# Reading the first expert's early rows two units sooner

## The chip, the cores and the metric

The program runs on one core of a Trainium2 chip. The metric is the time of one execution on the device, in microseconds (us). The kernel before took 737.21 us (median of 3 runs, 736.69 to 739.57).

## The reference

Three stages follow each other: an mLSTM over 4 batches, 8 heads and 768 steps; a mixture of 8 experts in which each of the 3072 tokens goes to the one expert with the highest logit; and a gated MLP over all tokens. Shortened, with the names of the reference:

```python
for t in range(S):                                   # mLSTM, per batch and head
    m_new = max(f_gate[t] + m, i_gate[t])
    f, i = exp(f_gate[t] + m - m_new), exp(i_gate[t] - m_new)
    C = f * C + i * outer(v[t], k[t]);  n = f * n + i * k[t]
    y[t] = sigmoid(o_gate[t]) * (C @ q[t]) / max(abs(n @ q[t]), 1)

logits = (x / |x|) @ (emb / |emb|).T / tau           # x: 3072 x 320
expert = argmax(logits);  gate = max(softmax(logits))
out[expert == e] = gate * (relu(x[expert == e] @ w1[e]) @ w2[e])   # 320 -> 1024 -> 320

h = x @ w_in;  result = (h * sigmoid(1.702 * h)) @ w_out           # 320 -> 2048 -> 320
```

## The kernel before, in words

**Units.** The mLSTM is cut into 24 units of 128 tokens (6 pieces of the sequence, 4 batches), worked on in one loop over `u` = 0 to 23; the last one, 23, and what follows it are written out behind the loop (the tail). Every engine runs its own queue in the order in which the code is written: nothing is reordered by a scheduler. In a unit, TensorE (PE) makes scores and products, VectorE (DVE) a scan and the elementwise work, ScalarE (ACT) copies, and GpSimd (POOL) the outputs `x` of a unit (`finish`) and the scatters.

**Routing.** Two units later a unit's rows are transposed (`route_t`), its 8 logits are made (`route_l`), and per batch of units come the one-hot of the best expert (`route_hot`), the rank inside the expert (`route_rank`, small matmuls into the single PSUM bank `r`), the slot (`route_slot`) and the running count of rows per expert (`route_cnt`). A `scatter` on POOL then writes the 128 rows of a unit to their slots in the DRAM tensor `rows`, which holds a region per expert. Scatters run behind by some units: `pend` holds those still to come.

**The first expert.** At `u` = 8 the expert with the most rows so far is named the first. Its first 256 rows (`EARLY`) are worked on ahead of the others: `early_load` reads them from `rows` into a buffer of SBUF, `early_x(c)` transposes them in three parts of 128 columns, `early_xhi` and `early_xlo` split each part into a rounded half (`xeh`) and the remainder (`xel`), and `early_mm(s, i0, i1)` makes the products of hidden block `s` (6 blocks of 128, 8 matmuls each: five with `xeh`, three with `xel`). `early_relu` makes their activations `he`. These products stand between the last routing steps of the tail.

**Sorting and the flag.** `order` sorts the experts by their counts, with some 20 short operations of DVE on 8 or 64 numbers, and writes `vals_i`: the experts in order, where their rows go, and a flag. The flag is 1 if an expert has more rows than was planned for it, or if the first expert had less than 256 rows when they were read (`enough`); then every engine takes a slow general path. All engines load the flag into a register and branch.

**Behind the sort.** `load_x0(1)` reads rows 256 to 511 of the first expert (tile `xr`), `early_o(m)` multiplies hidden block `m` by the second weights (6 matmuls each), then comes the branch, `touch` and the transposes of `xr` (`prep_x0`), and from there the experts one after the other. `xr` lies in memory that the first stage used; so its load waits for the last instructions that used that memory, among them the tiny ACT operation on `warm` that follows two table loads of ACT (one for the square root `rn` of the rows' norms, one for Exp).

In the loop the changed lines stand in this surrounding:

```python
for u in range(0, NU - 1):                 # NU = 24
    ...                                    # scores, scan, epilogues, routing of unit u - 2
    for i in range(0 if u < US else 1 if u < NU - 5 else 2):     # US = 10
        if pend:
            scatter(pend.pop(0))
```

Of the kernel before, what the change touches and what calls it, by code (L numbers as in the profile page):

```python
# [14 lines left out]
ALU = mybir.AluOpType  # L15
# [11 lines left out]
def kernel(ctx, tc, qT_in, kT_in, kvo_in, i_gate, f_gate, expert_emb, tau, w12, wio, out, dbg=None):  # L27
# [116 lines left out]
    with ExitStack() as actx:  # L144
# [116 lines left out]

        dC = ps_o.tile([P, G, 3 * DV], F32, tag="dC", name="dC")
        nc.vector.memset(dC, 0.0)
# [347 lines left out]

        def route_l(u, late=None):
# [6 lines left out]
            nc.tensor.matmul(lp, xT[:, 2], enT[:, 2], start=False, stop=True)  # L619
            if late in (None, 1):  # L620
# [31 lines left out]
        def route_hot(us):  # L652
            for _ in hot_steps(us):
                pass
# [17 lines left out]

        def route_cnt(us):
            oh, old, new = hot.pop(us[0])
            cs = wk.tile([P, E], F32, tag="cs", name="cs")
            nc.vector.tensor_reduce(out=cs, in_=oh.rearrange("p n e -> p e n"), axis=AX.X, op=ALU.add)
            nc.vector.tensor_tensor(out=new, in0=old, in1=cs, op=ALU.add)

        def route_slot(us, late=False):
# [64 lines left out]
        onehot = ap1.tile([P, E], F32, name="onehot")  # L744
        lack = const.tile([P, 1], F32, name="lack")

        def first():
# [14 lines left out]

        def enough(out):

            t = wk.tile([P, E], F32, tag="cs", name="cs")
            nc.vector.tensor_tensor(out=t, in0=early["n"], in1=onehot, op=ALU.mult)
            yield
            nc.vector.tensor_reduce(out=lack, in_=t, axis=AX.X, op=ALU.add)
            yield
            nc.vector.tensor_scalar(out=out, in0=lack, scalar1=-1.0, scalar2=float(EARLY), op0=ALU.mult, op1=ALU.add)  # L770
# [10 lines left out]
        def early_n():  # L781
            early["b"] = ps_o.tile([P, H, NI], F32, tag="ip", name="xt").rearrange("p h d -> p (h d)")

            early["n"] = early["b"][:, EARLY:EARLY + E]
            nc.tensor.matmul(early["n"], ones16, cnt[(nroute[0] - 1) % 2], start=True, stop=True)

        def early_x(c):
            if c == 0:
                early["h"] = wk.tile([P, 3, EARLY], F32R, tag="xeh", name="xeh", bufs=1)
                t = wk.tile([P, H, P], F32R, tag="wm", name="xel").rearrange("p h t -> p (h t)")  # L790
                early["l"] = t[:, 0:3 * EARLY].rearrange("p (c t) -> p c t", c=3)
            if c == 1:
                early["b"] = ps_o.tile([P, H, NW], F32, tag="op", name="xt").rearrange("p h d -> p (h d)")
            t = early["t", c] = early["b"][:, c // 2 * EARLY:(c // 2 + 1) * EARLY]
# [9 lines left out]
        def early_mm(s, i0=0, i1=8):  # L804
            if s == 0 and i0 == 0:
                early["p", 0] = ps_1.tile([P, H, P], F32, tag="sp", name="hp").rearrange("p h t -> p (h t)")[:, 0:EARLY]
            elif s == 1 and i0 == 0:
                early["p", 1] = dC.rearrange("p g f -> p (g f)")[:, 0:EARLY]
            elif 1 < s < 4 and i0 == 0:
                early["p", s] = ps_t.tile([P, G, P], F32, tag="pt", name="hp").rearrange("p a t -> p (a t)")[:, 0:EARLY]  # L810
            elif s == 4:
                early["p", s] = ps_o.tile([P, H, NW], F32, tag="op", name="hp").rearrange("p h d -> p (h d)")[:, 0:EARLY]
            elif s == 5:
                early["p", s] = ps_o.tile([P, H, NI], F32, tag="ip", name="hp").rearrange("p h d -> p (h d)")[:, 0:EARLY]
            h_seq(early["p", s], wslot[s][0], early["h"], early["l"], i0, i1)

        def early_relu(s):
# [11 lines left out]
            else:  # L829
                nc.vector.scalar_tensor_tensor(out=hl, in0=hp, scalar=0.0, in1=hh.bitcast(F32), op0=ALU.max, op1=ALU.subtract)  # L830

        def order_mm():
            early["a"] = r_bank(2)[:, 0:E]
            nc.tensor.matmul(early["a"], ones16, cnt[nroute[0] % 2], start=True, stop=True)

        def order():
# [10 lines left out]
            bg, q, m1, m2, m3, m4 = (sq(i, j) for i in range(2) for j in range(3))  # L847
            lacks = enough(cp[:, E:E + 1])
            nc.vector.tensor_copy(cn, early["a"])
            next(lacks)  # L850
            nc.vector.scalar_tensor_tensor(out=key, in0=cn, scalar=float(E), in1=key0, op0=ALU.mult, op1=ALU.add)
            tt(out=bg, in0=row(key), in1=col(key), op=ALU.is_gt)
            next(lacks)
            red(ordr, bg)
# [3 lines left out]
            tt(out=m3, in0=q, in1=row(cn), op=ALU.mult)  # L858
            next(lacks, None)
            red(cp[:, 0:E], m3)  # L860
# [11 lines left out]
        with tc.manual_schedule():  # L872
# [45 lines left out]
            for u in range(0, NU - 1):  # L918
# [117 lines left out]
            for i in pend:  # L1036
                scatter(i)
            early_load()
            pv(u - 1)
# [10 lines left out]
            assert next(steps, True)  # L1050
            keep_warm(dC.rearrange("p g f -> p (g f)"), 2)
            route_sq(u - 1)
# [7 lines left out]
            early_n()  # L1060
# [6 lines left out]
            early_x(0)  # L1067
            route_l(u, 1)
            route_rank(batch, 2)
            route_slot(batch, True)  # L1070
            route_cnt(batch)
            for i in batch:
                scatter(i)
            early_x(1)
            early_x(2)
            for c in range(3):
                early_xhi(c)
            nc.scalar.activation(out=rn, in_=ss_all.unsqueeze(2), func=AF.Sqrt)
            nc.scalar.activation(out=warm, in_=warm, func=AF.Exp)
            batch = [u]  # L1080
            route_hot(batch)
            early_mm(0, 0, 5)
            route_rank(batch, 2)
            early_xlo(0)
            route_slot(batch, True)
            route_cnt(batch)
            for i in batch:
                scatter(i)
            for c in range(1, 3):
                early_xlo(c)  # L1090
            for s in range(1, 4):
                early_mm(s, 0, 5)
                if s == 2:
                    order_mm()
# [631 lines left out]
```

## Time and profile before

| | |
|---|---|
| median of 3 runs | 737.21 us (736.69 to 739.57) |
| the profiled execution's own time | 739.55 us |
| its span, first to last instruction | 737.9 us |
| mean granted TensorE clock | 0.994 of full speed |
| the tail, from the last unit's scores to `touch` | 157.52 to 183.41 us of the span |
| PE busy in the span | 714.6 us (97%), 4767 matmuls |
| DVE, ACT, POOL busy | 515.3, 368.3, 237.6 us |

A row of the timeline reads: start, length, engine, line, operation, tiles (output, arrow, inputs), shape, number of instructions; in brackets, how long the engine sat idle ahead of it and what ended that. A row with more than one instruction runs from the first one's start to the last one's end. The granted clock (PEclk) of a stretch is a share of full speed.

### The profile page before, as it was taken

What the parts mean: (1) busy time and instruction counts of PE and PEld (TensorE: products, weight loads), DVE (VectorE), ACT (ScalarE), POOL (GpSimd) and SP (SyncE); (2) the same over time, 40 slices, a digit from 0 to 9 for tenths busy, and PEclk for the clock granted to TensorE, in tenths of its full rate; (3) what the DMA queues carried; (4) which work ended last, traced back from release to release, by engine and by line L of the source; (5) the groups of instructions that cost most, each with busy time, mean ns of one, the idle gap of its engine ahead of it and who ended that gap; (6) DMA issues with size and microseconds to landing.
All of it is one profiled execution on the core that took longest, in us unless ns stands there. A gap on an engine that the chain in (4) does not pass through costs nothing.

```text
span 737.9 us, 13402 instructions
## 1 busy us (share of the span) xinstructions
PE 714.6 (97%) x4767; PEld 669.6 (91%) x4767; DVE 515.3 (70%) x1080; ACT 368.3 (50%) x857; POOL 237.6 (32%) x353
## 2 busy tenths in 40 slices
PE   7999999997999999999999999999999999999994
PEld 5899899997989999999998888888888888889994
DVE  8778899985799998999867745545645544435542
ACT  4664555544666665767555443433333333334442
POOL 6674678873235433645210003003003003002011
PEclk9999999999999999999999999999999999999998
DMA  5689988822877768677721202202201201102000
GB/s 174 200 287 269 284 233 261 250 88 78 288 238 158 236 193 221 193 222 242 215 64 57 71 1 58 65 0 58 65 1 52 48 1 48 33 0 57 3 20 18
DMA packets 70106, 93.14 MB, mean 126 GB/s; under 512 B 31858, under 2 KB 56530, under 8 KB 70034
## 3 DMA queue, kind: packets, MB, share of 16 engines
q1 hardware_dynamic: 66818, 84.05, 39.3%
q0 software_dynamic: 3072, 7.89, 3.1%
q8 instruction: 38, 0.62, 0.4%
q14 instruction: 34, 0.28, 0.1%
q10 hardware_dynamic: 144, 0.30, 0.1%
HBM read 71.11 MB, written 17.18 MB: 120 GB/s over the span
## 4 chain that ended last, share of the span: by engine, by line
issue 43%; PE 24%; POOL 5%; DVE 2%; DMA 1%; POOLq 0%; ACT 0%; SPq 0%
PE acc L1225 12%; PE hp L139 11%; POOL out_dram L1270 3%; POOL xr L1381 2%; PE xt L1149 1%; DMA xr<-y 1%; DVE w L122 0%; POOL gap L1272 0%; DVE xl L1151 0%; DVE w L112 0%; DVE hs L1199 0%; DVE fr L1294 0%; PE xt L1165 0%; POOLq L1721 0%; DVE ex L1291 0%
## 5 line engine op out<-in xcount | busy, mean ns | idle before, releaser
L1225 PE MATMUL acc<-wout,hhl 128*128 128x320 f32 x1152 | 187.3, 309 | 0.0
L1225 PEld LDWEIGHTS acc<-wout,hhl 128*128 128x128 f32 x1152 | 175.9, 188 | 7.8 <-DVE o L1252 0.2
L1210 DVE TENSOR_TENSOR sg<-hp,sg 128x512 f32<-128x512 f32 (+1 forms) x112 | 68.9, 615 | 93.5 <-ACT sg L1209 85.9
L139 PE MATMUL hp<-xh,win 128*128 128x512 f32 (+1 forms) x560 | 131.1, 364 | 0.0
L1270 POOL DMA_INDIRECT out_dram<-o,tokd x24 | 24.0, 1002 | 312.9 <-ACT o L1254 309.2
L1209 ACT ACTIVATE sg<-hp 128x512 f32<-128x512 f32 (+1 forms) x112 | 60.4, 539 | 124.5 <-PE hp L139 121.9
L1212 DVE TENSOR_TENSOR hhl<-sg,hhl 128x512 fp32r<-128x512 f32 (+1 forms) x112 | 71.7, 640 | 70.3 <-ACT hhl L1211 69.8
L1225 PE MATMUL acc<-w,hs 128*128 128x320 f32 x636 | 104.3, 310 | 0.7 <-DVE hs L1199 0.7
L139 PEld LDWEIGHTS hp<-xh,win 128*128 128x128 f32 x560 | 93.8, 188 | 11.7 <-DVE sg L1210 0.3
L1211 ACT CAST hhl<-sg 128x512 fp32r<-128x512 f32 (+1 forms) x112 | 62.7, 559 | 80.5 <-DVE sg L1210 78.2
L1225 PEld LDWEIGHTS acc<-w,hs 128*128 128x128 f32 x636 | 96.8, 188 | 2.5 <-DVE hs L1199 1.0
L139 PE MATMUL hp<-xl,win 128*128 128x512 f32 (+1 forms) x336 | 85.7, 363 | 0.0
L111 POOL TENSOR_TENSOR w<-r,w 128x256 fp32r<-128x256 f32 x58 | 49.5, 853 | 102.9 <-ACT w L106 78.4
L139 PEld LDWEIGHTS hp<-xl,win 128*128 128x128 f32 x336 | 58.8, 189 | 11.0 <-DVE xl L1421 0.2
L139 PE MATMUL hp<-xh,w 128*128 128x440 f32 (+6 forms) x320 | 66.8, 338 | 0.0
L139 PEld LDWEIGHTS hp<-xh,w 128*128 128x128 f32 x320 | 51.4, 189 | 1.7
L1198 ACT ACTIVATE hs<-hp 128x440 fp32r<-128x440 f32 (+6 forms) x64 | 30.3, 473 | 38.2 <-PE hp L139 36.4
L479 PE MATMUL sp<-qT,kblk 120*128 120x128 f32 x384 | 47.1, 276 | 0.2 <-DVE wm L484 0.2
L479 PEld LDWEIGHTS sp<-qT,kblk 120*128 120x128 f32 x384 | 44.8, 192 | 0.9 <-issue 0.5
L542 PE MATMUL op<-vp_in,wm 128*128 128x96 f32 (+1 forms) x368 | 43.7, 272 | 0.0
L542 PEld LDWEIGHTS op<-vp_in,wm 128*128 128x128 f32 x368 | 42.9, 192 | 0.0
L139 PE MATMUL hp<-xl,w 128*128 128x440 f32 (+6 forms) x192 | 42.8, 331 | 0.0
(323 smaller groups left out, 1127.0 us busy)
## 6 DMA issues: line engine op xcount, KB each, us to landing
r<-in_w_dram SPq DMA_DIRECT2D x32, 704.0 KB
kvo<-in_kvo_dram SPq DMA_DIRECT2D x24, 480.0 KB
c<-in_wio_dram SPq DMA_DIRECT2D x16, 704.0 KB
fb<-dec SPq DMA_DIRECT2D x40, 128.0 KB
rows<-zt SPq DMA_DIRECT2D x8, 640.0 KB
qT<-in_qT_dram SPq DMA_DIRECT2D x24, 180.0 KB
xr<-y SPq DMA_DIRECT2D x5, 640.0 KB
kblk<-in_kT_dram SPq DMA_DIRECT2D x48, 60.0 KB
```

The source lines that it names most:

```text
L111: eng.tensor_tensor(out=t[:, 3 * P:5 * P].rearrange("p (c f) -> p c f", c=2), in0=r1[:, 0:2], in1=hif[:, 0:2], op=ALU.subtract)
L139: nc.tensor.matmul(hp, a, b, start=(i == 0), stop=(i == len(seq) - 1))
L479: nc.tensor.matmul(sp[:, h - hs.start], kblk[u % NLD][0:KR, h // 3, h % 3, :], qT[u][0:KR, h // 3, :], start=True, stop=True)
L542: nc.tensor.matmul(ops[:, h * NW:h * NW + n], wm[u][:, h], vp_in[u % NLD][:, h * DV:h * DV + n], start=True, stop=True)
L1198: nc.scalar.activation(out=hh, in_=hp, func=AF.Relu)
L1209: nc.scalar.activation(out=sg, in_=hp, func=AF.Sigmoid, scale=1.702)
L1210: nc.vector.tensor_tensor(out=g, in0=hp, in1=sg, op=ALU.mult)
L1211: nc.scalar.copy(hh, g)
L1212: nc.vector.tensor_tensor(out=hl, in0=g, in1=hh.bitcast(F32), op=ALU.subtract)
L1225: nc.tensor.matmul(acc_t[blk][i], hl if j == 2 else hh, w[:, DM:2 * DM] if j == 1 else w[:, 0:DM], start=(first and j == 0), stop=(last an ...
L1270: sc = nc.gpsimd.indirect_dma_start(out=out, out_offset=bass.IndirectOffsetOnAxis(ap=tokd[:, ti:ti + 1], axis=0), in_=o[:, i], in_offset=None)
L1381: eng.tensor_tensor(out=xr_t[blk], in0=xr_t[blk], in1=gated[:, t0:t0 + n].unsqueeze(2).to_broadcast([P, n, 3 * P]), op=ALU.mult)
```

## The change

- `early_load` moves from the tail (behind all scatters so far) to the end of the loop's body at `u` = 21, and reads into a buffer of the `kvo` pool that unit 20 has done with. By then the scatters of units 0 to 15 have been issued: on odd `u` from 11 to 17 the loop now issues two, and one from 18 to 21.
- `enough` moves from the sort to `u` = 20: a small matmul of the counts into bank `r` and three DVE operations that write `miss`. An ACT copy brings `miss` into the sort.
- In the tail, `early_x` takes the place of matmuls of the identity whose results nothing reads (`keep_warm`, L84), and parts of `early_mm` stand between the last logits. Units 22 and 23 get their one-hots one behind the other, then their ranks and slots.
- The square root `rn` and the Exp on `warm` move from ahead of the activations `early_relu` to behind them.
- The load of the flag moves behind `early_o`.

```diff
-        def enough(out):
+        def enough():
+            n = r_bank(None)[:, 0:E]
+            nc.tensor.matmul(n, ones16, cnt[nroute[0] % 2], start=True, stop=True)
             t = wk.tile([P, E], F32, tag="cs", name="cs")
-            nc.vector.tensor_tensor(out=t, in0=early["n"], in1=onehot, op=ALU.mult)
+            nc.vector.tensor_tensor(out=t, in0=n, in1=onehot, op=ALU.mult)
...
         def early_load():
-            t = pmb[0].rearrange("p h t -> p (h t)")
+            t = ld.tile([P, 3, H, D], F32, tag="kvo", name="er", bufs=4).rearrange("p a h d -> p (a h d)")
...
-                for i in range(0 if u < US else 1 if u < NU - 5 else 2):
+                for i in range(0 if u < US else 1 + u % 2 if u < 18 else 1 if u < NU - 2 else 2):
                     if pend:
                         scatter(pend.pop(0))
+                if u == NU - 4:
+                    enough()
+                if u == NU - 3:
+                    early_load()
...
             for i in pend:
                 scatter(i)
-            early_load()
...
+            early_x(0)
+            early_x(1)
+            early_xhi(0)
             route_t(u - 1)
-            keep_warm(dC.rearrange("p g f -> p (g f)"), 3)
-            sp_late.append(ps_1.tile([P, H, P], F32, tag="sp", name="sp_late"))
+            early_x(2)
+            early_mm_bank()
+            early_mm(0, 0, 2)
+            early_xhi(1)
+            early_xlo(0)
             route_l(u - 1, 0)
...
+            early_xhi(2)
+            early_mm(0, 2, 5)
+            route_l(u, 1, False)
+            route_rank(batch, 2)
+            old = route_cnt(batch)
+            early_xlo(1)
+            nc.vector.tensor_copy(logit_all[:, NTILE - 1], sp_late[0][:, 0, 0:E])
+            late = [u]
+            route_hot(late)
+            route_cnt(late, True)
+            hot[batch[0]] = old
+            route_slot(batch, True)
+            hot.pop(batch[0])
+            early_mm(2, 0, 5)
+            route_rank(late, 2)
+            early_mm(1, 0, 5)
+            order_mm()
+            early_xlo(2)
+            route_slot(late, True)
...
-            nc.scalar.activation(out=rn, in_=ss_all.unsqueeze(2), func=AF.Sqrt)
-            nc.scalar.activation(out=warm, in_=warm, func=AF.Exp)
...
             for s in range(WA):
                 early_mm(s, 5 if s < 4 else 0)
                 early_relu(s)
+            nc.scalar.activation(out=rn, in_=ss_all.unsqueeze(2), func=AF.Sqrt)
+            nc.scalar.activation(out=warm, in_=warm, func=AF.Exp)
...
             load_x0(1)
-            flag = nc.values_load(vals_i[0:1, 2 * E:2 * E + 1], min_val=0, max_val=1)
             acc_tiles(0)
             for m in range(WA // 2):
                 early_o(m, m == 0)
+            flag = nc.values_load(vals_i[0:1, 2 * E:2 * E + 1], min_val=0, max_val=1)
```

On ACT, at the end of the tail, the two table loads stood between the splits of the early rows (`xeh`) and the activations (`he`) in the kernel before:

```order
L799 CAST xeh<-xt 128x256 x3
L1078 ACT_TABLE_LOAD
L1078 ACTIVATE rn<-ss_all 128x24
L1079 ACT_TABLE_LOAD
L1079 ACTIVATE warm<-warm 1x1
L822 ACTIVATE he<-hp 128x256
L827 ACTIVATE hf<-hp 128x256
```

In the changed kernel the same place, up to the load of the flag, reads:

```order
L822 ACTIVATE he<-hp 128x256
L827 ACTIVATE hf<-hp 128x256
L822 ACTIVATE he<-hp 128x256 x2
L1102 ACT_TABLE_LOAD
L1102 ACTIVATE rn<-ss_all 128x24
L1103 ACT_TABLE_LOAD
L1103 ACTIVATE warm<-warm 1x1
L1538 TENSOR_LOAD vals_i
```

The two table loads and `warm` are now ACT's last work ahead of the branch.

On PE, in the tail from the logits of unit 21 (`ip<-enT,xT`) to those of unit 22 (`op<-enT,xT`), the kernel before had:

```order
L617 MATMUL ip<-enT,xT 128x128
L618 MATMUL ip<-enT,xT 128x128
L619 MATMUL ip<-enT,xT 128x128
L84 MATMUL dC<-ident 128x128 x2
L586 MATMUL pr<-ident,x 128x128
L587 MATMUL pr<-ident,x 128x128
L588 MATMUL pr<-ident,x 128x128
L84 MATMUL dC<-ident 128x128 x3
L617 MATMUL op<-enT,xT 128x128
```

In the changed kernel, where `er` is the early rows' buffer:

```order
L618 MATMUL ip<-enT,xT 128x128
L619 MATMUL ip<-enT,xT 128x128
L620 MATMUL ip<-enT,xT 128x128
L796 MATMUL dC<-ident,er 128x128 x4
L587 MATMUL pr<-ident,x 128x128
L588 MATMUL pr<-ident,x 128x128
L589 MATMUL pr<-ident,x 128x128
L796 MATMUL xt<-ident,er 128x128 x2
L139 MATMUL sp_late<-xeh,w 128x256 x2
L618 MATMUL op<-enT,xT 128x128
```

All six transposes of the early rows and the first two products stand where five matmuls of `keep_warm` stood.

On PE, at the flag, the kernel before had:

```order
L139 MATMUL hp<-xel,w 128x256 x3
L139 MATMUL hp<-xeh,w 128x256 x5
L139 MATMUL hp<-xel,w 128x256 x3
L1531 TENSOR_LOAD vals_i
L1225 MATMUL acc<-w,he 128x320 x18
```

The changed kernel has:

```order
L139 MATMUL hp<-xel,w 128x256 x3
L139 MATMUL hp<-xeh,w 128x256 x5
L139 MATMUL hp<-xel,w 128x256 x3
L1229 MATMUL acc<-w,he 128x320 x18
L1538 TENSOR_LOAD vals_i
```

The 18 matmuls of `early_o` no longer stand behind the load of the flag.

## Rows read from the trace of the kernel before

**Rows 1.** Timeline of PE in the tail.

```profile
168.80 0.44 PE L796 MATMUL xt<-ident,pmb 128*128 128x128 f32 x2 [1.74 <-DMA pmb<-rows]
...
173.41 0.75 PE L139 MATMUL hp<-xeh,w 128*128 128x256 f32 x5
...
174.72 0.52 PE L139 MATMUL hp<-xel,w 128*128 128x256 f32 x3
...
180.09 2.88 PE L1225 MATMUL acc<-w,he 128*128 128x320 f32 x18 [1.88 <-DVE vals_i L868]
183.41 0.41 PE L1173 MATMUL xt<-ident 128*128 128x64 f32 x2 [0.45 <-PEq L1535]
183.65 0.88 PE L1165 MATMUL xt<-ident,xr 128*128 128x128 f32 x6
```

**Rows 2.** Busy time (PE PEld DVE ACT POOL), PEclk, DMA share, GB/s by microsecond.

```profile
170.00:171.00 1.00, 1.00 (x9) 1.00 (x8) 0.79 (x7) 0.00 (x0) 0.89 (x2) 0.50 0.00 0
...
173.00:174.00 1.00, 1.00 (x10) 0.96 (x10) 0.96 (x6) 0.98 (x3) 0.79 (x3) 1.00 0.18 67
...
178.00:179.00 1.00, 0.20 (x2) 0.00 (x0) 1.00 (x3) 0.52 (x2) 1.00 (x2) 1.00 0.58 210
179.00:180.00 1.00, 0.00 (x0) 0.00 (x0) 0.97 (x8) 0.00 (x0) 0.09 (x1) 1.00 0.00 0
180.00:181.00 1.00, 0.91 (x6) 0.94 (x7) 0.50 (x2) 0.21 (x1) 0.00 (x0) 1.00 0.00 0
```

**Rows 3.** Timeline at units 15 to 17, all engines.

```profile
114.97 0.72 POOL L577 TENSOR_TENSOR sg<-sg,dn 128x320 f32<-128x320 f32 x1 [1.24 <-DVE dn L570]
...
118.24 0.83 PE L493 MATMUL dC<-vp_in,kw 128*120 128x123 f32 x6 [0.32 <-POOL kw L470]
...
120.80 0.17 DVE L621 COPY logit_all<-r 128x8 f32<-128x8 f32 x1 [0.49 <-PE r L619]
```

**Rows 4.** Timeline of DVE at unit 20 and in the tail.

```profile
145.44 0.12 DVE L621 COPY logit_all<-r 128x8 f32<-128x8 f32 x1
...
165.56 0.49 DVE L580 TENSOR_TENSOR x<-num,sg 128x320 f32<-128x320 f32 x1
...
170.87 0.15 DVE L639 TENSOR_REDUCE mx<-logit_all 128x1 f32<-128x8 f32 x1
...
171.74 0.42 DVE L802 TENSOR_TENSOR xel<-xt,xeh 128x256 fp32r<-128x256 f32 x1
...
175.39 0.17 DVE L849 COPY spare<-r 128x8 f32<-128x8 f32 x1 [1.28 <-PE hp L139]
...
179.37 0.14 DVE L866 TENSOR_SCALAR vals_i<-spare 128x1 int32<-128x1 f32 x1
```

**Rows 5.** Timeline of POOL: scatters.

```profile
149.15 1.01 POOL L695 DMA_INDIRECT rows<-x,slot_i  x1 [0.16 <-issue]
...
158.03 0.96 POOL L695 DMA_INDIRECT rows<-x,slot_i  x1 [2.22 <-DVE cs L676]
...
173.64 0.96 POOL L695 DMA_INDIRECT rows<-x,slot_i  x1 [0.21 <-issue]
```

**Rows 6.** Timeline of ACT from the table loads on, and one wait behind the branch.

```profile
171.82 1.28 ACT L1078 ACT_TABLE_LOAD   x1
...
174.64 0.20 ACT L1079 ACTIVATE warm<-warm 1x1 f32<-1x1 f32 x1
...
177.66 0.96 ACT L822 ACTIVATE he<-hp 128x256 fp32r<-128x256 f32 x2
...
202.63 0.51 ACT L106 CAST w<-r 128x384 fp32r<-128x384 f32 x1 [0.84 <-DMA r<-in_w_dram]
```

**Rows 7.** Timeline of SP's DMA issues (x2: second ends last).

```profile
165.64 0.43 SPq L778 DMA_DIRECT2D pmb<-rows  x1
...
176.52 8.74 SPq L1127 DMA_DIRECT2D xr<-rows  x2
...
198.18 6.95 SPq L97 DMA_DIRECT2D r<-in_w_dram  x3
```

More of the change, by code (lines that the diff above doesn't have):

```diff
@@ L610, with route_l @@
         sp_late = []
-        def route_l(u, late=None):
+        def route_l(u, late=None, copy=True):
             b, c = units[u]
@@ L619, in route_l @@
             nc.tensor.matmul(lp, xT[:, 2], enT[:, 2], start=False, stop=True)
+            if not copy:
+                return
             if late in (None, 1):
@@ L671, in route_rank, with route_cnt @@
             rp_t[us[0]] = rk
-        def route_cnt(us):
-            oh, old, new = hot.pop(us[0])
+        def route_cnt(us, keep=False):
+            oh, old, new = hot[us[0]] if keep else hot.pop(us[0])
             cs = wk.tile([P, E], F32, tag="cs", name="cs")
@@ L677, in route_cnt @@
             nc.vector.tensor_tensor(out=new, in0=old, in1=cs, op=ALU.add)
+            return oh, old, new
         def route_slot(us, late=False):
@@ L761, in first @@
             nc.vector.tensor_copy(first_i, lead[0:1])
[L763 removed]
+        def enough():
+            n = r_bank(None)[:, 0:E]
+            nc.tensor.matmul(n, ones16, cnt[nroute[0] % 2], start=True, stop=True)
             t = wk.tile([P, E], F32, tag="cs", name="cs")
[L766 to L767 removed]
+            nc.vector.tensor_tensor(out=t, in0=n, in1=onehot, op=ALU.mult)
             nc.vector.tensor_reduce(out=lack, in_=t, axis=AX.X, op=ALU.add)
[L769 to L770 removed]
+            nc.vector.tensor_scalar(out=miss, in0=lack, scalar1=-1.0, scalar2=float(EARLY), op0=ALU.mult, op1=ALU.add)
         early = {}
         def early_load():
[L775 removed]
+            t = ld.tile([P, 3, H, D], F32, tag="kvo", name="er", bufs=4).rearrange("p a h d -> p (a h d)")
             early["r"] = t[:, 0:EARLY // P * 3 * P].rearrange("p (i d) -> p i d", d=3 * P)
@@ L779, in early_load @@
             nc.sync.dma_start(out=early["r"][:, :, DM:3 * P], in_=src[:, :, 2 * P:DM])
[L781 to L785, printed above, removed]
         def early_x(c):
@@ L791, in early_x @@
                 early["l"] = t[:, 0:3 * EARLY].rearrange("p (c t) -> p c t", c=3)
-            if c == 1:
-                early["b"] = ps_o.tile([P, H, NW], F32, tag="op", name="xt").rearrange("p h d -> p (h d)")
-            t = early["t", c] = early["b"][:, c // 2 * EARLY:(c // 2 + 1) * EARLY]
+            if c < 2:
+                t = early["t", c] = dCb[:, c * EARLY:(c + 1) * EARLY]
+            else:
+                t = early["t", c] = ps_o.tile([P, H, NI], F32, tag="ip", name="xt").rearrange("p h d -> p (h d)")[:, 0:EARLY]
             for i in range(EARLY // P):
@@ L805, in early_mm @@
             if s == 0 and i0 == 0:
-                early["p", 0] = ps_1.tile([P, H, P], F32, tag="sp", name="hp").rearrange("p h t -> p (h t)")[:, 0:EARLY]
+                early["p", 0] = sp_late[0][:, 4:8].rearrange("p a t -> p (a t)")[:, 0:EARLY]
             elif s == 1 and i0 == 0:
-                early["p", 1] = dC.rearrange("p g f -> p (g f)")[:, 0:EARLY]
+                early["p", 1] = dCb[:, 0:EARLY]
             elif 1 < s < 4 and i0 == 0:
@@ L830, in early_relu, with early_mm_bank @@
                 nc.vector.scalar_tensor_tensor(out=hl, in0=hp, scalar=0.0, in1=hh.bitcast(F32), op0=ALU.max, op1=ALU.subtract)
+        def early_mm_bank():
+            sp_late.append(ps_1.tile([P, H, P], F32, tag="sp", name="sp_late"))
         def order_mm():
-            early["a"] = r_bank(2)[:, 0:E]
+            early["a"] = sp_late[0][:, 1, 0:E]
             nc.tensor.matmul(early["a"], ones16, cnt[nroute[0] % 2], start=True, stop=True)
@@ L847, in order @@
             bg, q, m1, m2, m3, m4 = (sq(i, j) for i in range(2) for j in range(3))
-            lacks = enough(cp[:, E:E + 1])
+            nc.scalar.copy(cp[:, E:E + 1], miss)
             nc.vector.tensor_copy(cn, early["a"])
-            next(lacks)
             nc.vector.scalar_tensor_tensor(out=key, in0=cn, scalar=float(E), in1=key0, op0=ALU.mult, op1=ALU.add)
             tt(out=bg, in0=row(key), in1=col(key), op=ALU.is_gt)
-            next(lacks)
             red(ordr, bg)
@@ L1065 @@
             route_hot(batch)
-            route_sq(u)
[L1067 to L1077, printed above, removed]
-            nc.scalar.activation(out=rn, in_=ss_all.unsqueeze(2), func=AF.Sqrt)
-            nc.scalar.activation(out=warm, in_=warm, func=AF.Exp)
[L1080 to L1094, printed above, removed]
+            early_xhi(2)
[17 more added lines that the diff above has]
+            route_slot(late, True)
+            hot.pop(late[0])
+            for i in batch + late:
+                scatter(i)
+            route_sq(u - 1)
+            route_sq(u)
+            early_mm(3, 0, 5)
             order()
```

8 lines of the change are left out of this document (3 added, 5 removed).

## The prediction

> **What bounds the kernel now.** I read the timeline of the tail engine by engine, PE first, then the same microseconds as a table, and then the queues that feed it. From 183.65 us on, PE goes through the experts almost without a pause, so what the change can give or take is the moment at which the transposes of `xr` begin there [rows 1]. In the tail ahead of it PE stands still three times: 1.74 us for the early rows (`pmb<-rows`), 1.88 us for `vals_i`, 0.45 us at the branch [rows 1]. After the first of these its clock is at the lower level (granted 0.50 at 170 us, 1.00 again at 173); after the second it stays at 1.00 [rows 2]. The three stalls and the slow stretch are what there is to win: 4.1 us, and some 1.5 us.
>
> All sums are against the profiled execution (span 737.9 us, 739.55 with what lies around it, 1.65 us). The median of the runs, 737.21, lies 2.34 below; I add the change in the span to the median.
>
> **Step 1, `enough` at unit 20: +0.9 us.** Its matmul writes bank `r`, of which there is one, so PE waits until DVE has copied the logits out of it, and the scores of unit 21 stand behind it. In the trace that copy ends at 145.56 [rows 4]. DVE then waits for the matmul and runs three dependent operations. Five dependent ones of this size took 0.87 us until the next could start (170.87 to 171.74) [rows 4]; three are 0.5, and the matmul's way there and back I put at 0.4 (an estimate: the copy of the sort waits 1.28 us for such a matmul [rows 4], but with others queued ahead of it). DVE is the engine without idle time in the loop, so I take the whole 0.9 (bounds 0.5, the three alone, and 1.8, with that 1.28). What leaves the sort, the same three operations, stood in gaps between dependent ones and gives back 0.1 at most; I count nothing.
>
> **Step 2, scatters: +0.3 us.** One is added on POOL in each of units 11, 13, 15 and 17, at 1.2 us (0.96 and 0.21 of idle ahead [rows 5]) and a short memset. Behind unit 15 POOL had 1.24 us of idle time, and the chain POOL, PE, DVE that follows shows waits at each link (0.32 and 0.49 us) [rows 3]. So the added scatter overshoots by its memset and the next start, about 0.3, and that reaches DVE. Bounds 0 and 0.6 (if unit 17 does it again). Units 19 to 21 lose one each, where DVE is the bound, which gives nothing.
>
> **Step 3, the early rows: their wait goes.** The last scatter ahead of the load is unit 21's, at 149.15. From the issue of a scatter to the next load that waits for it the trace shows 2.9 us (173.64 to 176.52) [rows 5, 7], and from that load's issue to PE 3.2 (165.64 to 168.80) [rows 1, 7]. So the load leaves at 152 and the rows are there at 155.3 (156.5 with steps 1 and 2), 10 us ahead of PE. The scatters of units 16 to 19 now wait for this load's end, but before they waited for DVE's slots already, until 158.03 [rows 5], 159.2 after; so that new wait costs nothing, and `finish` of unit 22, queued behind them on POOL, moves with steps 1 and 2 only. The six transposes and two products on PE take the place of five `keep_warm` matmuls.
>
> **Step 4, to the sort: 2.4 us earlier.** The last `x` is ready at 166.05 [rows 4], after: 167.25. From there DVE holds 26 short operations and three `xel` (0.42 each) until the copy that begins the sort. The short ones lie 0.08 (independent) to 0.2 (dependent) apart; I take 0.17, as most are chains: 4.4 + 1.3 = 5.7, so 172.95 instead of 175.39 [rows 4]. Bounds: 2.1 and 5.2 for the short ones, that is 3.4 to 6.5. PE is not the bound there, but it must wait: the rank of unit 23 needs bank `r`, which is free only when DVE has read unit 22's rank, 1.0 us before the sort, at 172.0. Two groups of five products and the count are queued behind it, 0.75 each [rows 1], so the products with `xel` begin at 173.5 instead of 174.72: 1.2 us earlier. PE idles about 1.5 us ahead of 172.
>
> **Step 5, behind the hidden products.** ACT's activations end 1.2 us earlier, 177.4 instead of 178.62 [rows 6]. Before, PE's products ended 1.88 us ahead of 180.09, at 178.2; after, it goes from 177.0 straight into `early_o` and is through at 179.9 instead of 183.0. The load of the flag (0.6, from its write at 179.51 to PE's next start) and the branch (0.45) bring `touch` to 180.95 instead of 183.41 [rows 1, 4].
>
> **Step 6, what is late next: `xr`.** Its load waits for ACT's operation on `warm`. Before, `warm` was done at 174.84 and the load left at 176.52, with the last scatter. Now the two table loads follow the activations: from the first to the end of `warm` 3.02 us [rows 6], so 180.4, and the load leaves at 180.5. The load before was in by 179.0, since no bytes move in the next microsecond [rows 2, 7]: 2.3 us. So PE gets `xr` at 182.9 instead of 183.65: **0.75 us earlier** is all that is left of 2.5.
>
> [...]
>
> **Step 7, the clock: +1.5 us.** PE then has nothing from 179.9 to 182.9 but `touch`: 3 us nearly idle. A wait of 1.74 was followed by the lower level, one of 1.88 was not [rows 1, 2]. I take it that 3 us are. The level lasted some 3 us before; PE is the bound behind 183, so half of that is lost: 1.5. Bounds 0 and 3 (a second one after the 1.5 us idle at 171, whose loss would also shift ACT and `xr`).
>
> **Sum.** -0.75 + 1.5 = +0.75 in the span: 738.65, or 740.3 with what lies around it; on the median, **737.9 us**. That is no change: this kernel's runs tell apart about 0.5%, 3.7 us.
>
> **Rivals.**
> 1. *The clock stays up* (for it: 1.88 us did no harm; against: the new wait is longer). Only the 0.75 is left: 736.5 us.
> 2. *`xr` is not held by ACT*, and PE keeps the 2.5 us of step 5, and more if step 4 runs at its lower bound (2.3): gain 2.5 to 4.8, 733.6 us in the middle. Against it: the table loads are plainly behind the activations; for it only that the sum of short operations is loose.
> 3. *Slower, the SP queue.* SP reads the flag after it has issued the load of `xr`, then waits for that load's end in the branch, and only then issues the other half of `xr` and the weights. Before, it read the flag at 179.5 and the second half left at 184.8 (the end of the merged row, 185.26, less the 0.43 of an issue) [rows 4, 7]: 5.3 us of a branch and of queue work. Now it reads at 180.9, 1.4 late; if the work behind the branch counts from the end of the load, 182.8, it is 3.3 late. The weights issued at 198.18 become 199.6 to 201.5 [rows 7], and ACT already waited 0.84 us for them at 202.63 [rows 6]. Nothing covers a later one but the 0.75 by which PE is late itself. This decides as soon as SP is later than PE by more than that; price 0.6 to 2.5 on top of the forecast: 739.5 us.
>    [...] The trace shows the gap on SP, not its cause.
> 4. *Both idle stretches pull the clock down*, the one at 171 too: 1.5 us more than forecast, 739.4.
> 5. *The change does not do what it says.* The flag is now taken from the counts of 16 units. Counted with the reference's inputs, the expert with the most rows in units 0 to 3 has 258 rows after unit 15, and 256 are wanted. The flag stays down by two rows. If it went up, the general path would repeat six hidden blocks (0.75 and 0.52 each [rows 1]) and two loads of 3.2: 14 us at the least, 751 or more.
>
> **How the numbers follow.** Forecast 0.38; rival 1 0.24; rival 2 0.09; rival 3 0.16; rival 4 0.12; rival 5 0.01. The likeliest one's own range is 736.4 to 739.6 (steps 1 and 2 each at their bounds, and the runs' spread). For 8 in 10 I reach to rivals 1, 3 and 4 and half of rival 2: 734.3 to 740.9. Faster by over 0.5% is below 733.5: half of rival 2 and a little of 1, 0.07. Slower by over 0.5% is above 740.9: the upper ends of 3 and 4 together, 0.10. The rest, 0.83, is no change.
>
> **What would show it.** Step 1: a gap of PE ahead of the scores of unit 21, and the last `x` 1.2 us later. Step 3: no wait of PE on the early rows, and scatters of unit 22 that start with DVE's slots. Step 4: the copy of the sort near 173, with a wait of PE for DVE about 1.5 us long. Step 6: `xr` leaves right after `warm`, near 180.5, and PE's longest wait of the tail is on that load. Step 7: the granted clock at 0.5 for some 3 us from 183 on. The forecast is wrong if `xr` leaves before 178, or if PE begins the transposes of `xr` before 181 or after 185.

## The result and the profile after

The changed kernel takes 743.04 us (median of 13 runs, 741.08 to 745.71), the kernel before in the same comparison 737.76 (13 runs): ratio 1.0067, 95% interval 1.0052 to 1.0081, so 4.9 us slower (3.8 to 6.0). The forecast was no change, 737.9 us. The profiled execution has a span of 741.2 us, 3.3 more than that of before.

The timeline of PE in the tail, which answers to [rows 1] (start, us, what ran, in brackets the idle time before it and what ended it):

```profile
173.12 0.17 PE L667 MATMUL r<-base,ones 128*128 128x8 bf16 x1 [1.32 <-DVE rk_all L693]
...
177.87 2.79 PE L1229 MATMUL acc<-w,he 128*128 128x320 f32 x18
181.12 0.41 PE L1177 MATMUL xt<-ident 128*128 128x64 f32 x2 [0.45 <-PEq L1539]
184.57 1.51 PE L1169 MATMUL xt<-ident,xr 128*128 128x128 f32 x6 [3.05 <-DMA xr<-rows]
185.74 4.80 PE L1229 MATMUL acc<-w,he 128*128 128x320 f32 x18
190.38 0.68 PE L139 MATMUL hp<-xh,w 128*128 128x160 f32 x5
```

No wait for the early rows and none for `vals_i`: `early_o` runs 177.87 to 180.66 and the touch stands at 181.12 instead of 183.41. But then PE waits 3.05 us for `xr`, and six transposes and 18 products behind that wait take 1.51 and 4.80 us; the transposes took 0.88 before [rows 1]. The same microseconds as a table (busy time of PE, PEld, DVE, ACT, POOL, then the granted clock, the DMA share and GB/s) say why:

```profile
180.00:182.00 2.00, 1.07 (x7) 0.70 (x5) 0.06 (x1) 1.48 (x2) 0.00 (x0) 1.00 0.02 4
182.00:184.00 2.00, 0.00 (x0) 0.00 (x0) 0.00 (x0) 0.00 (x0) 0.00 (x0) 0.79 0.53 168
184.00:186.00 2.00, 1.43 (x7) 1.46 (x8) 0.20 (x1) 0.90 (x3) 0.00 (x0) 0.50 0.02 4
...
188.00:190.00 2.00, 2.00 (x9) 2.00 (x9) 0.00 (x0) 0.00 (x0) 0.00 (x0) 0.50 0.82 201
190.00:192.00 2.00, 2.00 (x19) 2.00 (x18) 0.23 (x1) 0.30 (x1) 0.00 (x0) 1.00 0.92 354
```

The granted clock is at the lower level, 0.50 of full speed, until 190 us. What held `xr` stands on ACT and SP (their timelines; [rows 6, 7] before):

```profile
178.07 0.39 ACT L822 ACTIVATE he<-hp 128x256 fp32r<-128x256 f32 x1 [0.32 <-PE hp L139]
178.47 1.28 ACT L1102 ACT_TABLE_LOAD   x1
...
181.29 0.20 ACT L1103 ACTIVATE warm<-warm 1x1 f32<-1x1 f32 x1
```

```profile
181.63 5.51 SPq L1131 DMA_DIRECT2D xr<-rows  x2
```

`warm` ends at 181.49 and the load leaves 0.14 us later, as the forecast's step 6 had it, only 1.1 us later than it had it. In the loop, the timelines of POOL and of PE:

```profile
126.53 0.96 POOL L699 DMA_INDIRECT rows<-x,slot_i  x1 [0.21 <-issue]
...
135.33 1.01 POOL L699 DMA_INDIRECT rows<-x,slot_i  x1 [4.80 <-DVE cs L679]
...
136.41 0.73 POOL L578 TENSOR_TENSOR sg<-sg,dn 128x320 f32<-128x320 f32 x1
```

```profile
138.87 0.33 PE L587 MATMUL pr<-ident,x 128*128 128x128 f32 x1 [0.99 <-POOL x L581]
147.61 0.17 PE L771 MATMUL r<-cnt,ones 128*128 128x8 bf16 x1 [0.26 <-DVE logit_all L624]
```

With two scatters in units 11, 13, 15 and 17, the one of unit 12 comes to POOL's head in unit 18, before DVE has made its slots: POOL stands 4.80 us, the gates of the next unit stand behind it, and PE waits 0.99 us for `x`. The test of the flag costs what step 1 said. DVE goes on at 148.28, 0.89 us after the copy at 147.39 began, where before it went on 0.03 us after it; the last `x` is there at 168.05 (DVE):

```profile
147.39 0.17 DVE L624 COPY logit_all<-r 128x8 f32<-128x8 f32 x1 [0.28 <-PE r L620]
...
148.28 0.49 DVE L555 TENSOR_TENSOR num<-ip,ei_tok 128x328 f32<-128x328 f32 x1
...
167.56 0.49 DVE L581 TENSOR_TENSOR x<-num,sg 128x320 f32<-128x320 f32 x1
```

### The profile page after: what moved, and what is told of

It is laid out like the page before. It is cut to its first block, busy times and chain, and to the rows that moved or that the text cites. A ratio compares the mean times of both kernels' runs of the same rounds, so it can differ in the third digit from the quotient of the medians.

```text
span 741.2 us, 13389 instructions
## 1 busy us (share of the span) xinstructions
PE 715.2 (96%) x4757; PEld 670.0 (90%) x4757; DVE 514.7 (69%) x1080; ACT 368.6 (50%) x858; POOL 234.2 (32%) x353
## 4 chain that ended last, share of the span: by engine, by line
issue 42%; PE 24%; POOL 5%; DVE 2%; DMA 1%; POOLq 0%; ACT 0%; SPq 0%
PE acc L1229 12%; PE hp L139 11%; POOL out_dram L1274 3%; POOL xr L1385 2%; PE xt L1153 1%; DMA xr<-y 1%; DMA xr<-rows 0%; DVE w L122 0%; DVE w L112 0%; POOL gap L1276 0%; PE xt L1169 0%; DVE xl L1155 0%; DVE hs L1203 0%; POOLq L1725 0%; DVE ex L1295 0%
## 5 line engine op out<-in xcount | busy, mean ns | idle before, releaser
L139 PEld LDWEIGHTS hp<-xh,win 128*128 128x128 f32 x560 | 93.9, 188 | 11.5 <-ACT xh L1424 0.2
```

The source lines that it names most:

```text
L139: nc.tensor.matmul(hp, a, b, start=(i == 0), stop=(i == len(seq) - 1))
```

## Where the time went, by three stretches

To compare executions that start their loop a little earlier or later, three stretches are read from the timelines of each: A, the add of `num` of unit 10 to that of unit 22; B, that of unit 23 to the first transpose of `xr`; C, from there to the first product `hp<-xh,w`. All in us.

| run | A loop | B tail | C behind `xr` | granted clock below 1.00 in these |
|---|---|---|---|---|
| before, the profiled one | 72.92 | 19.80 | 3.36 | 169 to 173 (in B) |
| before, once more (b0) | 75.59 | 16.61 | 3.36 | 89 to 93 (in A) |
| before, with filler (b1) | 74.62 | 17.85 | 3.36 | none |
| before, flag test (x2) | 75.07 | 17.05 | 3.36 | none |
| before, scatters (x1) | 75.33 | 16.05 | 3.36 | none |
| before, `warm` late (e4) | 73.92 | 19.78 | 4.58 | 183 to 186 (in C) |
| changed | 75.00 | 19.19 | 5.81 | 183 to 190 (in C) |
| changed, once more (a2) | 75.34 | 19.42 | 5.99 | 183 to 189 (in C) |
| changed, filler (x3b) | 74.76 | 19.26 | 3.33 | none |
| changed, warm early (e1) | 74.48 | 15.98 | 3.36 | none |
| h2 | 73.64 | 15.93 | 3.36 | none |

The tail of the one execution on which the forecast was summed is the outlier: in the four others of that kernel and its variants that don't wait for `xr`, B is 16.1 to 17.9. From the same start to the touch alone it takes 19.56 us there, 16.37 in b0 and 15.8 to 17.6 in b1, x1, x2 and e4; the changed kernel takes 15.74. So against b0 the change wins 0.6 us at the touch, where the forecast had 2.5.

Against b1 the changed kernel loses 0.4 in A, 1.3 in B and 2.45 in C; against b0's B, 2.6. That is 4.2 to 5.4 us, and 4.9 were measured. These are single executions, and A of one and the same program lay 3 us apart in two of them (77.74 in x3, 74.76 in x3b), so that A can't carry much and the fit of the total is in part luck. In b1 1.1 us of B is a longer wait at the branch, 1.57 us instead of 0.45, whose cause stays open.

## The experiments

**e1: `warm` back in front.**

```diff
             route_sq(u)
+            nc.scalar.activation(out=rn, in_=ss_all.unsqueeze(2), func=AF.Sqrt)
+            nc.scalar.activation(out=warm, in_=warm, func=AF.Exp)
             early_mm(3, 0, 5)
...
-            nc.scalar.activation(out=rn, in_=ss_all.unsqueeze(2), func=AF.Sqrt)
-            nc.scalar.activation(out=warm, in_=warm, func=AF.Exp)
```

> The changed kernel with the square root and the warm-up exponential put back ahead of the activations of the hidden products (into the 4.08 us in which ACT waits there), nothing else. Theory A (the load of xr waits for the warm-up, and the wait that follows pulls PE's clock down): the load leaves with the last scatter, near 177.5 us instead of 181.63, PE begins the transposes of xr some 0.25 us after its touch at 181.1, so near 181.4 instead of 184.57 (3.2 us earlier), and the granted clock stays at 1.00 behind them (another 2.45 us that the transposes and early products took longer). Span 735.5, time 737.4 us: 5.6 less than the changed kernel, no different from the kernel before. Theory B (the loss comes from the loop, which ends 2.0 us later, and from the SP queue): PE would still be late after the branch; at most 1 us of gain, 742 us or more.

Measured: 736.89 us, 0.9992 of before (0.9974 to 1.0011). PE:

```profile
180.35 0.41 PE L1177 MATMUL xt<-ident 128*128 128x64 f32 x2 [0.45 <-PEq L1539]
180.59 0.88 PE L1169 MATMUL xt<-ident,xr 128*128 128x128 f32 x6
181.23 2.89 PE L1229 MATMUL acc<-w,he 128*128 128x320 f32 x18
```

`warm` ends at 173.27, the load leaves at 176.66, there is no wait behind the touch and the clock stays at 1.00. By the ratios (1.0067 and 0.9992) two lines of ACT are worth 5.5 us, 5.6 were expected: theory A holds, B falls.

**e4: the mirror, `warm` moved behind the activations in the kernel before.**

> The kernel before with the square root and the warm-up exponential moved behind the activations of the hidden products, as the changed kernel has them; nothing else. Theory A: the activations end near 177.0 instead of 178.6 if ACT begins them when the products are there (they wait for 0.69 us already), the two table loads follow, the warm-up ends at 181 to 181.7, the load of xr leaves there instead of 176.52, and PE gets xr at 184 to 184.7 instead of 183.65; after the wait of 1 us or less behind the branch the clock stays up: 0.5 to 1 us slower, or 3 to 3.5 us slower if the clock does fall. Theory B: no change against the kernel before, 737.8 us.

Measured: 742.19 us, 1.0056 (1.0035 to 1.0077): 4.1 us slower. PE:

```profile
179.80 0.41 PE L1173 MATMUL xt<-ident 128*128 128x64 f32 x2 [0.45 <-PEq L1535]
183.34 1.51 PE L1165 MATMUL xt<-ident,xr 128*128 128x128 f32 x6 [3.13 <-DMA xr<-rows]
184.51 3.57 PE L1225 MATMUL acc<-w,he 128*128 128x320 f32 x18
```

The same wait, the same lower clock behind it. That PE would wait 1 us or less was wrong: the touch came at 179.80, since in this execution there was no wait for `vals_i` either.

**e3 and x3, x3b: filler in the wait for `xr`.**

```diff
             nc.tensor.matmul(t[:, 0:n], ident, ident[:, 0:n], start=True, stop=True)
+            keep_warm(t, 24)
```

> The changed kernel with 24 products of the identity with itself (128 columns, some 0.11 us each, result unused) on PE behind the touch, while it waits for xr; nothing else. Theory A (of the loss 2.45 us are PE's clock, which falls in the wait of 3.05 us): the granted clock is 1.00 from 184 to 190 us, the transposes of xr still begin near 184.6, and six transposes and 18 products take 0.9 and 2.9 us instead of 1.5 and 4.8: 740.6 us, 2.4 less than the changed kernel. Rival (the products behind the wait are slow for another cause, such as transfers or ACT's reads): they stay slow, 743 us.

Measured: 742.22 us, 1.0053 (1.0034 to 1.0073). The 24 products are 48 instructions in the trace: the filler took 5.58 us and ran 2.2 us past the load, so this run says only that the 18 products behind it take 2.89 us at a clock of 1.00. With 12:

> The changed kernel with 12 products of the identity with itself behind the touch (24 instructions of 0.11 us, since a product in fp32 is two; 2.8 us in all, result unused), so that they end before xr is there; the 24 products tried before took 5.6 us and ran 2.2 us past it. Theory A: the granted clock stays at 1.00 up to and behind the transposes of xr, which begin when the load is there as in the changed kernel; 18 products take 2.9 us: 1.2 to 2.5 us less than the changed kernel, 740.5 to 741.8. If the clock's part of the loss was misread: 743.

Measured: 743.06 us in six runs, 1.0078 (1.0056 to 1.0100): no gain. The profile had the 18 products at 2.89 us, but its A was 77.74, with the clock at 0.50 near 91 us. So it was run again beside the changed kernel:

> The changed kernel itself, once more, beside the filler and the two combinations on one chip. 1.0067 of the kernel before, as in the first comparison; granted clock at the lower level for several us behind the wait for xr.

> The changed kernel with 12 products of the identity behind the touch, again, now beside the changed kernel on the same chip. In the first look its 18 products behind xr took 2.9 us instead of 4.8 at a clock of 1.00, yet six runs gave 1.0078 of the kernel before, with a loop that ran 3 us late in the profiled one. Theory A: the clock's 2.4 us are real and the first medians were the loop's scatter between runs: 1.2 to 2.5 us less than the changed kernel here. Rival: what the clock gives back is lost elsewhere (the chain behind xr ends no earlier): the same as the changed kernel.

Measured on one chip: the changed kernel 743.26 us, 1.0072 (1.0047 to 1.0096); the filler 741.32, 1.0037 (1.0019 to 1.0055): 2.6 us less by the ratios, 1.9 by the medians, and the intervals overlap. PE of x3b:

```profile
181.56 2.90 PE L84 MATMUL xt<-ident 128*128 128x128 f32 x24
184.82 0.84 PE L1169 MATMUL xt<-ident,xr 128*128 128x128 f32 x6 [0.36 <-DMA xr<-rows]
185.42 2.89 PE L1230 MATMUL acc<-w,he 128*128 128x320 f32 x18
```

The load comes no earlier than in the changed kernel; what is gained is C, 3.33 instead of 5.81. So that the clock costs 2.4 us behind `xr` is shown by the traces: with filler the 18 products take 2.89 us in all three profiles, and the rival, another cause for their slowness, falls. That the whole time gets them back is not shown: one of the two comparisons has the gain, the other none, and their ratios lie 3 us apart.

**x1: the scatter pattern alone, in the kernel before.**

```diff
-                for i in range(0 if u < US else 1 if u < NU - 5 else 2):
+                for i in range(0 if u < US else 1 + u % 2 if u < 18 else 1 if u < NU - 2 else 2):
```

> The kernel before with the changed kernel's pattern of scatters in the loop (two in units 11, 13, 15 and 17, one in 18 to 21) and nothing else. Theory C (the pattern costs the loop 1 to 2 us: POOL stands behind the scatter of unit 12 until DVE has made its slots, and short operations of DVE that run beside a scatter take longer): POOL waits some 4.8 us for DVE near 130 us as in the changed kernel, PE waits some 1 us on x, and the time is 1 to 2 us more than the kernel before: 739 to 740. The forecast's term: 0.3 us, no difference that can be told. Theory D (the test of the flag at unit 20 is the loop's loss): no difference.

Measured: 738.94 us, 1.0028 (1.0011 to 1.0044), 2.0 us slower by the ratio (0.8 to 3.2). POOL:

```profile
135.16 1.01 POOL L695 DMA_INDIRECT rows<-x,slot_i  x1 [5.48 <-DVE cs L676]
```

PE waits 0.99 us for `x` as in the changed kernel. The forecast's 0.3 lies outside the interval. The trace shows less than the runs: its A is 0.7 us longer than b1's. Of short operations of DVE that take longer beside a scatter, the first profile of before has a case: L568 on `dn` took 0.41 us at 139.47, beside the scatter of 138.95, where its median is 0.17.

**x2: the test of the flag alone, in the kernel before** (the product and the three DVE operations of `enough` at unit 20).

> The kernel before with the test of the flag at unit 20 added as the changed kernel has it (one product into bank r, three operations of DVE; its result is unused, and the test in the sort stays). The forecast's term: the copy of unit 18's logits to the operation behind the test takes 0.9 us more, PE's scores of unit 21 begin 0.2 to 0.4 us late, time 0.9 us more than the kernel before: 738.7. Theory D: 1.5 us or more. Theory C: 0.5 to 0.9.

Measured: 737.43 us, 1.0005 (0.9987 to 1.0023). It can't be told from nothing, nor from 0.9.

**e2: the scatter of unit 12 a unit later.**

```diff
-1 + u % 2 if u < 18 else 1 if u < NU - 2 else 2
+1 + u % 2 if u < 18 else 0 if u == 18 else 2 if u == 19 else 1 if u < NU - 2 else 2
```

> The changed kernel with the scatter of unit 12 issued in unit 19 (two there) instead of unit 18, nothing else. Theory C (the extra scatters, and above all this one, which sits on POOL for 4.80 us until DVE has made its slots and holds the gates of the next unit behind it, are the loop's loss, not the test of the flag): POOL's wait of 4.8 us and PE's 0.99 us on x go, the loop's end comes 1 to 1.5 us earlier; but the load of xr still waits for the warm-up, so the gain passes on: 741.5 to 742 us. Theory D (the test of the flag at unit 20 is the loop's loss, the stall on POOL is covered): less than 0.3 us, 743 us.

Measured: 741.28 us, 1.0036 (1.0022 to 1.0050), 2.3 us less than the changed kernel by the ratios. PE's wait of 0.99 us for `x` is gone, and from unit 16 to unit 22 of stretch A it takes 36.80 us instead of 37.64; POOL still stands 4.32 us there, now ahead of the gates. C of this execution is 4.59 instead of 5.81, which the edit doesn't touch: the clock was up again sooner (it had fallen in the loop too, from 89 to 93 us). So the trace shows 0.84 us for the edit, and what more the runs gained stays open.

**g0 and g1: e1 and e2 together; and with PE's order changed.**

> The changed kernel with the square root and the warm-up ahead of the hidden products' activations and the scatter of unit 12 in unit 19. The two edits alone gave 0.9992 and 1.0036 of the kernel before, where the changed kernel had 1.0067. If they add (one frees xr, the other the loop): 0.9992 - 0.0031 = 0.996, some 735 us. If POOL's stall is hidden once PE no longer waits for xr: 0.999.

> As the combination, and PE's products of the second and fourth chunk put ahead of the last rank, with the count in bank r: PE's wait of 1.31 us for the last one-hot goes, the early products end 1.3 us earlier, and the transposes of xr begin when its load is there, 0.8 to 1.2 us earlier than in the combination: 0.9945 of the kernel before, some 734 us. If the sort or the last scatter (the load of xr) is the bound instead, no gain over the combination.

Measured: g0 737.31 us, 0.9983 (0.9965 to 1.0001); g1 738.50, 1.0006 (0.9989 to 1.0023). The edits of g0 don't add: on top of e1, e2's edit is worth 0.0009 (0.7 us) and not 0.0031, which is the 0.84 us that it saved in A. g1 did begin the transposes of `xr` 0.54 us earlier than g0 (B 15.43 and 15.97), and in its profile lost it to the next load, whose wait g0 doesn't have (PE of g1):

```profile
179.47 0.88 PE L1169 MATMUL xt<-ident,xr 128*128 128x128 f32 x6
...
186.48 0.44 PE L1169 MATMUL xt<-ident,xr 128*128 128x128 f32 x2 [0.83 <-DMA xr<-rows]
```

SP issued the other half of `xr` 7.4 us after the first, in g0 5.7. Why stays open; it is the forecast's third rival, met in another kernel.

**f1: four edits at once.**

> The changed kernel with four edits: the square root and the warm-up exponential ahead of the hidden products' activations; the scatters in the loop as the kernel before has them up to unit 21, the early rows' load one unit later behind the scatter of unit 15, and the last two scatters of the loop's batch behind the gates; the flag's product in the bank that unit 22's ranks use, copied by ACT, with its three DVE operations where DVE waits for the last values; and the products of chunk 2 ahead of the last rank, so that PE doesn't stand for the last one-hot. Expected, from the first edit alone at 0.999 of the kernel before: 1.5 us from the loop, 1.0 from the PE order: xr transposes near 178.5, no wait of POOL over 2.5 us in the loop, 734.5 to 735.5 us, 0.3 to 0.5% faster than the kernel before. If the loop's losses are jitter of the loads and not the change's: 736.5.

Measured: 738.82 us, 1.0020 (0.9996 to 1.0044): not faster. Its profile has the low clock near 92 us, and PE waits 0.84 us for `x` behind the scatters, 0.54 for the other half of `xr` and 1.99 for weights.

**b0 and b1: was the profiled execution of before a usual one?** b1 has `keep_warm(..., 7)` ahead of `early_x(0)`.

> The kernel before, one more profile. If its first profiled execution was a rare one: PE waits 1 to 2 us for the early rows as there, but the granted clock stays at 1.00, the sort's operations take 0.22 us each and end before PE is through with the hidden products, so there is no wait of 1.88 us for vals_i, and from the end of the wait for the rows to the touch it takes 11.5 to 11.7 us instead of 14.6. If it was a usual one: the clock falls again and vals_i is late again.

> The kernel before with 7 products of the identity (14 instructions, 1.5 us, result unused) on PE ahead of the transposes of the early rows, in its wait for them. If the clock falls there in a part of the executions only (about a quarter of the runs of the kernel before have a mean clock of 0.994 or less and lie 2 us above the rest): those go, the median moves by 0.5 us or so: 0.999, and no run has the low clock. If it falls in most: 0.997. If the clock there doesn't matter to the time: 1.000.

Measured: b0 739.50 us in its one run; b1 738.30, 1.0013 (0.9993 to 1.0032): filling that wait gives nothing that can be told. PE of b0:

```profile
171.03 0.44 PE L796 MATMUL xt<-ident,pmb 128*128 128x128 f32 x2 [1.22 <-DMA pmb<-rows]
...
179.25 2.80 PE L1225 MATMUL acc<-w,he 128*128 128x320 f32 x18
182.49 0.41 PE L1173 MATMUL xt<-ident 128*128 128x64 f32 x2 [0.45 <-PEq L1535]
```

From the end of the wait to the touch 11.5 us, where the first profile had 14.6 [rows 1], and no wait for `vals_i`. The sort tells why. DVE in the first profile of before, then in b0, then POOL in the one and the other:

```profile
176.32 0.77 DVE L856 TENSOR_TENSOR spare<-spare,e 128x64 f32<-128x64 f32 x1
177.15 0.65 DVE L858 TENSOR_TENSOR spare<-spare 128x64 f32<-128x64 f32 x1
...
179.66 0.18 DVE L868 CAST vals_i<-vf 128x16 int32<-128x16 f32 x1
```

```profile
176.37 0.22 DVE L856 TENSOR_TENSOR spare<-spare,e 128x64 f32<-128x64 f32 x1
176.63 0.22 DVE L858 TENSOR_TENSOR spare<-spare 128x64 f32<-128x64 f32 x1
...
177.88 0.21 DVE L868 CAST vals_i<-vf 128x16 int32<-128x16 f32 x1
```

```profile
176.28 2.81 POOL L828 TENSOR_TENSOR he<-hf,he 128x256 fp32r<-128x256 f32 x4 [1.59 <-ACT hf L827]
```

```profile
177.22 2.92 POOL L828 TENSOR_TENSOR he<-hf,he 128x256 fp32r<-128x256 f32 x4 [0.36 <-ACT hf L827]
```

In the first profile, with PE at the lower clock, the sort began 6.6 us after the rows were there (175.39 and 168.80, [rows 1, 4]), in b0 4.4 (175.44 and 171.03). So in the first profile it ran beside POOL's operations, which there began at 176.28 and in b0 at 177.22; the same DVE operation (L856) took 0.77 us beside them and 0.22 where they had not begun, another (L858) 0.65 and 0.22. Why they take longer beside POOL no run shows. b0 lost its clock elsewhere, in the loop, behind a wait of 1.95 us for a copy of ACT's that was itself queued behind a wait for weights (PE, then its windows, columns as above):

```profile
88.20 0.44 PE L441 MATMUL tri<-rhsB,lhsA 96*64 96x512 f32 x1 [1.95 <-ACT pmb L434]
```

```profile
88.00:90.00 2.00, 1.77 (x8) 1.46 (x9) 1.45 (x6) 2.00 (x9) 0.31 (x1) 0.71 0.92 288
90.00:92.00 2.00, 2.00 (x11) 2.00 (x11) 1.78 (x6) 1.14 (x4) 1.92 (x4) 0.50 0.91 270
```

So the total came again (739.5, above the median as the first), the tail did not. That low clocks in the wait for the rows make up the scatter of before was wrong: five of b1's 12 runs still have a mean clock of 0.994 or less.

**h1 and h2: a version that keeps the gain.** h1 is e1 with the scatters `1 if u < 18 else 2`; h2 adds the flag's product in the bank of unit 22's ranks, copied by ACT, its three DVE operations in DVE's wait for the last values.

> The changed kernel with the square root and the warm-up ahead of the hidden products' activations, and with scatters one a unit up to unit 17 and two from unit 18 on, which still brings the scatter of unit 15 out in unit 21 ahead of the early rows' load; none waits for slots that DVE hasn't made. If the pattern costs 2 us, as the kernel before with it showed (1.0028): 0.9992 - 0.0025 = 0.9965 of the kernel before, no wait of POOL over 2 us between 125 and 140 us, and unit 10 to unit 22 take 73 us instead of 74.5 to 75. If two scatters in unit 18 cost as much: 0.999.

> As h1, and the flag's product in the bank of unit 22's ranks, copied by ACT, its three DVE operations in DVE's wait for the last values instead of at unit 20. The test alone cost the kernel before 1.0005 (0.35 us): 0.996 if that is had back, the same as h1 if not.

Measured: h1 736.77 us, 0.9987 (0.9971 to 1.0002); h2 735.44, 0.9974 (0.9956 to 0.9992): 1.9 us faster than before (0.6 to 3.2) and some 0.9% faster than the changed kernel. h1 missed its first expectation (0.9965): taking the pattern out of e1 gave 0.4 us and not 2, and A is 74.08 and not 73. h2's step beyond h1 is not clear of the noise, and h2 is the best of six versions, measured in one comparison. POOL of h2:

```profile
130.36 1.66 POOL L703 DMA_INDIRECT rows<-x,slot_i  x1 [0.21 <-issue]
...
133.91 0.72 POOL L578 TENSOR_TENSOR sg<-sg,dn 128x320 f32<-128x320 f32 x1 [1.80 <-DVE sl__1866 L693]
```

In the loop no scatter waits for slots any more, and POOL waits 1.80 us where it stood 4.80; the one at 158.81, in the tail, still waits 4.72.

## Why the prediction was wrong

The mechanism was found ahead, and the forecast's own signs came out in kind: the test of 0.9 us, PE's wait for DVE of about 1.5 (1.32), `xr` leaving right after `warm`, PE's longest wait of the tail on that load, the lower clock from 183 on. Their sizes did not: the last `x` came 2.0 us later and not 1.2, the sort at 174.10 and not near 173, and the lower clock lasted 7 us and not 3. It is the sum that failed. Of the 5.1 us between 737.9 and 743.04, steps 6 and 7 have 2.6, and adding to the median has the other 2.5:

- **"I add the change in the span to the median."** The sum for the span was +0.75; the two profiled executions differ by 3.3 and the medians by 5.3, since the first lay 2.34 above its median and the changed kernel's 0.14 below its own (742.90 and 743.04). The 4.1 us of stalls and the 1.5 of slow clock in [rows 1, 2] were taken for what there is to win. In b0, x1 and x2 the wait for `vals_i` isn't there and the clock is up in the tail, so their B was already 2.8 to 3.8 us shorter than the one shown, and b1's 2.0. The text gave the 2.34 us and didn't ask in which rows they were. The total alone would not have told: b0's is as high with another tail, and in the first profile a loop 1.7 us shorter than b1's balanced part of the longer tail.
- **Step 6 (`xr` at 182.9; it was 184.57).** Of the 1.7 us, 1.1 is the end of `warm`, at 181.49 instead of 180.4: 0.8 of it the loop (the last `x` was there at 168.05, not 167.25) and 0.3 step 4's short operations (6.05 us from there to the sort, not 5.7); the two table loads with their operations took the 3.02 us that were counted (178.47 to 181.49). So the activations began 0.4 us earlier than before and ended 0.16 earlier, where step 5 had 1.2. The other 0.6 is the load, 2.9 us from its issue to PE and not 2.3; the 2.3 was read from the end of its bytes (176.52 to 179.0, which is up to 2.5), while step 3 had 3.2 from issue to PE for a load of the early rows. The 0.75 us that were left of the gain became a loss of 0.92.
- **Step 7 (+1.5; it was 2.45).** The level lasted 7 us and not 3. Nearly all that PE did for 5.8 us behind the wait ran at it, and PE was the bound there: half of some 5 us. Rival 1, the clock stays up, is excluded by both profiles of this kernel. Rival 4 is out too: behind the wait of 1.32 us at 173 the clock stayed at 1.00.
- **Step 2 (+0.3).** Measured alone it is 2.0 (0.8 to 3.2) by the runs and 0.7 by stretch A against b1; taken out of e1 it gives 0.7 (g0) and 0.4 (h1), neither clear of the noise. The price was taken from a scatter's length and POOL's idle time; that the scatter of unit 12 would find no slots yet was not asked, though [rows 5] show exactly such a wait at 158.03, and I used it in step 3.
- **Step 1 (+0.9)** was right in the trace and is not seen in the time (x2).

Rival 2's 733.6 us presumed that `xr` isn't held; e1 shows what that would have given: 736.9, no gain that can be told, because the gain was counted from a tail that the other profiles don't have. Rival 3 (SP) and rival 5 (the flag) didn't decide: SP's weights left 1.2 us later than before, at 199.34, while PE was 3.4 later itself.

How much of step 2 the loop really loses stays open, between 0.4 and 2.0 us; so does what makes SP's second load late in g1, and how often before's tail looks like its first profile: one of its two has it.

## What to carry to other kernels

Before you price a stall, ask whether the profiled execution is a usual one, row by row and not by its total: take a second profile, since a stall that only one execution has can't be won. When work is put off to where its engine looks idle, follow what waits for its last instruction: two ACT operations of 0.2 us, with their table loads 3.02 us, held a load, the load held PE for 3.05 us, and PE's clock, at 0.50 behind that wait, added 2.45. A queue entry that is moved ahead must not come ahead of its input: the scatter of unit 12 kept POOL standing for 4.80 us.

## What the runs showed of the hardware

- Waits of PE of 3.0 to 3.3 us, behind the touch, were followed by the lower clock (0.50) in all four profiles that had them, for 3 to 7 us. Waits of 1.7 to 2.0 us were followed by it sometimes (1.74 in the first profile of before, 1.75 in e2, 1.76 in x3, 1.95 in b0) and sometimes not (1.76 in the changed kernel, 1.82 in x2, 1.88 in the first profile of before, 1.94 in x3b); those of e2, x3, b0, the changed kernel and x3b are one and the same wait, near 88 us in the loop. A filler that keeps PE busy to within 0.4 us of its data kept the clock at 1.00 (x3b).
- The lower level ended after different times for much the same wait: behind 3.05, 3.27, 3.01 and 3.13 us the 18 products took 4.80, 4.98, 3.58 and 3.57 us (changed twice, e2, e4).
